# Odd raw weight pieces staged in the turning buffers; the last conversions and the MLP's first half block in one go in slot 21

## The chip, the core and the metric

The kernel runs on one core of a Trainium2 chip. The metric is the device time of one execution in microseconds (us). Runs of one kernel differ by a few us, so results are quoted as medians with their range, and as ratios with a 95% interval.

"Cold" below means that the clock granted to TensorE is half of full, "warm" or "at speed" that it is full. Names: PE is TensorE, PEld its weight loads, DVE VectorE, ACT ScalarE, POOL GpSimd, SP SyncE. L426 is line 426 of the kernel before; in the changed kernel and its variants the numbers can be the same or shifted by one to four.

## The reference

Threshold attention on 8 batches x 8 heads x 576 rows x 64 columns, then a GELU MLP:

```python
scores = scale * (q @ k.T)
thresh = max(scores, axis=-1) - tau
scores = where(scores >= thresh, scores, -1e9)
attn   = softmax(scores)
x      = (attn @ v) as 4608 rows of 512
out    = gelu(x @ w_in) @ w_out           # w_in 512 x 2048, w_out 2048 x 512
```

The weights arrive as 64-bit floats. The kernel turns them into fp32 itself, in 32 pieces of 128 x 512.

## The kernel before

The work is a sequence of 160 *slots*. Slot n = 5p + i handles row tile i of head pair p; four pairs make a batch, so slots 0 to 19 are batch 0, 20 to 39 batch 1. A slot computes scores on PE, reduces, exponentiates and thresholds them (the *softmax*), and turns the result so that it can be multiplied with v. In batch 0 the turning is done on PE; from slot 20 on DVE transposes 32 x 32 blocks into two *turning buffers* `pd`, which are stored to DRAM and fetched back:

```python
pd = [const.tile([P, 4 * KR, P], FP32, name=f"pd{e}") for e in range(2)]
...
def turn_p(p, i):
    ...
    for e in range(n):
        to = pd_tail[p % 2] if i == NC else pd[e][:, :, i * Q:(i + 1) * Q]
        nc.vector.transpose(to[:, 0:NB, :], w[...])
    if i == NC - 1:                      # fourth tile of a pair: store both buffers
        for e in range(2):
            for a in range(4):
                nc.sync.dma_start(s["turned"][e, :, :, a * P:(a + 1) * P], pd[e][a * Q:(a + 1) * Q])
```

The tile of slot n - 1 is turned in slot n, so the buffers are stored in the slots 24, 29, 34 and written again from slots 26, 31, 36 on.

A raw piece is loaded twice by GpSimd, once shifted by three bytes, and converted in steps that alternate between DVE and ACT:

```python
if k % 2 and k < EARLY_PIECES:           # EARLY_PIECES = 24
    room = pd[k // 2 % 2]...             # odd early pieces: staged in a turning buffer
    raw, shifted = room[:, 0:2 * PIECE], room[:, 2 * PIECE:4 * PIECE]
else:                                    # the others: two buffers of the x pool (7 buffers)
    raw, shifted = (xg.tile([P, 2 * PIECE], U32, tag="x", name=s) for s in ("raw", "shifted"))
nc.gpsimd.dma_start(raw, src...)
nc.gpsimd.dma_start(shifted..., src...)
...
vec.tensor_scalar(expo, hi, 0x7FF00000, ...)                 # piece k + 1   0.42 us
nc.scalar.activation(power, expo, AF.Relu, ...)              # piece k + 1   0.72 us
vec.tensor_scalar(mant, top, ...)                            # piece k       0.42 us
vec.scalar_tensor_tensor(power, hi, ..., power, ...)         # piece k       0.69 us
vec.scalar_tensor_tensor(dst, mant, ..., power...)           # piece k       0.69 us
load_piece()                                                 # piece k + 4
```

Steps of the MLP are *filled* in between the slots. A block of 256 rows is 64 `hT` matmuls (two instructions each), a gelu on ACT after every eight of them, and 32 `o_ps` matmuls:

```python
for n in range(len(slots) + WEIGH + 1):
    ...
    scores(p, i); softmax_head(p, i)                 # scores, max, exp
    if 0 < p <= HP and i == 1:
        weigh_v(p - 1, 1); weighed = p               # turned softmax times v, copied to x by ACT
    if 0 < n <= len(slots): turn_p or turn_p_early of slot n - 1
    ...
    if p < NP: softmax_tail(p, i, batch < 2)         # threshold, sum, scaling
    ...
    if batch == 0:
        convert(EARLY_PIECES * 2100 / BATCH)
    elif n < BATCH + 2:
        convert(1e12 if n > BATCH else 9000)         # the last eight pieces, slots 20 and 21
    if batch:
        share = ...
        if batch == 1:
            share = BLK_NS / 8 if n < BATCH + 4 else (share * BATCH - BLK_NS / 2) / (BATCH - 4)
        fill(share, weighed // HP)
    if 0 < p <= HP and i == 0:
        weigh_v(p - 1, 0)
```

## Time and profile before

| | |
|---|---|
| time | 1517.32 us, median of 3 (1515.79 to 1517.84) |
| span of the profiled execution | 1520.2 us |
| PE busy | 1442.4 us (95%) |
| DVE busy | 900.2 us (59%) |
| ACT busy | 640.4 us (42%), with 147 table loads of 1.28 us |

The prediction below shows where PE waits and what ended each wait.

One thing about this trace matters for every later comparison. It has a wait for a load of k at its start that a second trace of the same kernel does not have. PE, in order of time (start, us, instruction, count, idle before and its releaser), first in the profiled execution above:

```profile
30.95 0.36 PE L256 MATMUL tr<-ident,k 64*128 64x64 f32 x1 [3.15 <-DMA k<-in_k_dram]
```

and in the second trace (run `before_2` below):

```profile
28.04 0.27 PE L256 MATMUL tr<-ident,k 64*128 64x64 f32 x1 [0.26 <-DMA k<-in_k_dram]
```

Where two traces are compared below, I therefore count from the start of slot 4's scores, which lies after this wait.

### The profile page before, as it was taken

The page shows a single profiled execution, that of the slowest core. Times are in us where ns is not written, and L with a number is a line of the kernel's source. Part 1 is how long each engine was busy: PE and PEld are TensorE (multiplying, and loading weights), DVE is VectorE, ACT ScalarE, POOL GpSimd, SP SyncE. Part 2 cuts the span into 40 slices and gives each one's busy share as a digit, 9 for nine tenths or more (in the row PEclk, how much of TensorE's full clock was granted, in tenths as well). Part 3 has the DMA queues.
Part 4 walks back from the last instruction along what each step waited for, and adds up shares of the span by engine and source line. Part 5 has one row for each costly group of instructions (what it writes and reads, how often), then busy time and mean ns, then how long its engine had stood idle before and what let it go on. Part 6 is the DMA issues. An engine that isn't in the chain of part 4 may idle for free.

```text
span 1520.2 us, 17439 instructions
## 1 busy us (share of the span) xinstructions
PE 1442.4 (95%) x6092; PEld 899.0 (59%) x6092; DVE 900.2 (59%) x2089; ACT 640.4 (42%) x932; POOL 41.3 (3%) x84
## 2 busy tenths in 40 slices
PE   5877588999999999999999999999999999999998
PEld 3544454656666565656565656575757474765764
DVE  6998566676666676676677766666666676000000
ACT  5766353763445343536252635362626262100110
POOL 3121100000000000000000000000000000000000
PEclk9797798999999999999999999999999999999999
DMA  9875447776666667685777776666666655400000
GB/s 264 249 228 148 160 111 199 192 179 170 170 174 176 183 162 183 165 206 145 193 180 182 186 182 181 175 171 156 165 177 179 173 151 146 134 14 7 7 14 14
DMA packets 398887, 237.61 MB, mean 156 GB/s; under 512 B 230352, under 2 KB 380880, under 8 KB 391632
## 3 DMA queue, kind: packets, MB, share of 16 engines
q1 hardware_dynamic: 391632, 202.96, 51.9%
q0 software_dynamic: 7168, 33.54, 6.5%
q8 instruction: 49, 0.80, 0.2%
q14 instruction: 38, 0.31, 0.1%
HBM read 144.43 MB, written 92.01 MB: 156 GB/s over the span
## 4 chain that ended last, share of the span: by engine, by line
PE 86%; DVE 6%; issue 3%; SPq 2%; ACT 2%; DMA 2%; POOL 0%; POOLq 0%; ACTq 0%; DVEq 0%
PE hT L426 33%; PE o_ps L437 32%; PE sc L320 11%; PE xT L398 9%; DVE p L345 2%; DVE nmx L331 1%; DVE power L174 1%; DMA turned<-pd 1%; DVE w_in L176 1%; DMA k<-in_k_dram 1%; SPq L228 1%; ACT p L332 1%; SPq L224 1%; DVE expo L165 0%; SPq L373 0%
## 5 line engine op out<-in xcount | busy, mean ns | idle before, releaser
L426 PE MATMUL hT<-x,w_in 128*128 128x256 f32 x2304 | 524.0, 385 | 16.4 <-ACT x L407 14.3
L437 PE MATMUL o_ps<-w_out,g 128*128 128x512 f32 x1152 | 515.8, 599 | 0.0
L426 PEld LDWEIGHTS hT<-x,w_in 128*128 128x128 f32 x2304 | 437.3, 192 | 105.2 <-issue 25.9
L331 DVE TENSOR_REDUCE nmx<-sc 128x1 f32<-128x576 f32 x288 | 206.3, 752 | 305.2 <-PE sc L320 304.1
L437 PEld LDWEIGHTS o_ps<-w_out,g 128*128 128x128 f32 x1152 | 215.2, 191 | 259.5 <-issue 255.8
L332 ACT ACTIVATE p<-sc,nmx 128x576 f32<-128x576 f32 x288 | 202.6, 740 | 332.7 <-DVE nmx L331 332.4
L345 DVE SCALAR_TENSOR_TENSOR p<-sc,thr,p 128x576 f32<-128x576 f32 x288 | 220.1, 796 | 11.1 <-ACT p L332 9.9
L320 PE MATMUL sc<-kT,qT 64*128 64x288 f32 x1024 | 186.3, 456 | 30.4 <-DVE p L345 29.9
L320 PEld LDWEIGHTS sc<-kT,qT 64*128 64x128 f32 x1024 | 103.4, 197 | 115.5 <-issue 96.2
L368 DVE STREAM_TRANSPOSE pd<-p 128x576 f32<-128x576 f32 x224 | 162.0, 757 | 13.8 <-DMA turned<-pd 13.5
L398 PE MATMUL xT<-pT,v 128*64 128x288 f32 x1280 | 167.8, 416 | 0.0
L430 ACT ACTIVATE g<-hT 128x512 f32<-128x512 f32 x144 | 84.9, 597 | 126.0 <-PE hT L426 125.1
L398 PEld LDWEIGHTS xT<-pT,v 128*64 128x64 f32 x1280 | 90.5, 140 | 77.8 <-issue 20.5
L356 DVE TENSOR_SCALAR p<-p,rden 128x576 f32<-128x576 f32 x216 | 103.6, 518 | 4.2
L430 ACT ACT_TABLE_LOAD x74 | 94.9, 1283 | 12.7 <-PE hT L426 11.6
L332 ACT ACT_TABLE_LOAD x73 | 93.7, 1283 | 3.1 <-DVE nmx L331 1.7
L407 ACT COPY x<-xT 128x256 f32<-128x256 f32 (+7 forms) x128 | 29.2, 284 | 150.4 <-PE xT L398 150.4
L440 ACT COPY o_sb<-o_ps 128x512 f32<-128x512 f32 x36 | 21.0, 583 | 147.4 <-PE o_ps L437 147.4
L354 ACT ACTIVATE p<-p,rden 128x576 f32<-128x576 f32 x72 | 52.3, 769 | 61.7 <-DVE rden L350 61.5
L320 PE MATMUL sc<-kT,q_tail 128*128 128x288 f32 x128 | 42.0, 454 | 13.0 <-DVE p L345 13.0
L320 PEld LDWEIGHTS sc<-kT,q_tail 128*128 128x128 f32 x128 | 22.9, 198 | 30.3 <-issue 26.4
L335 DVE TENSOR_SCALAR thr<-nmx,tau_eff 128x2 f32<-128x2 f32 (+1 forms) x160 | 36.2, 226 | 5.7
(65 smaller groups left out, 420.9 us busy)
## 6 DMA issues: line engine op xcount, KB each, us to landing
pT<-turned SPq DMA_DIRECT2D x56, 1440.0 KB, 8.0
turned<-pd SPq DMA_DIRECT2D x224, 320.0 KB, 5.2
out_dram<-o_sb SPq DMA_DIRECT2D x36, 256.0 KB, 2.2
turned<-pd_tail SPq DMA_DIRECT2D x112, 80.0 KB, 2.9
q<-in_q_dram SPq DMA_DIRECT2D x112, 72.0 KB, 9.0
k<-in_k_dram SPq DMA_DIRECT2D x112, 72.0 KB, 3.2
v<-in_v_dram SPq DMA_DIRECT2D x168, 40.0 KB, 2.2
raw<-in_moe_w_out_dram POOLq DMA_DIRECT2D x12, 512.0 KB, 3.9
```

What stands on the lines that cost most here:

```text
L320: nc.tensor.matmul(sc[e][:, h, 0:HALF], lhsT=lhsT, rhs=s["kT"][rows, at:at + HALF], start=True, stop=True)
L331: nc.vector.tensor_reduce(nmx[:, e:e + 1], sc, axis=AXIS.XY, op=ALU.max, negate=True)
L332: nc.scalar.activation(w[:, e * S:(e + 1) * S].rearrange("p (h s) -> p h s", h=2), sc, AF.Exp, bias=nmx[:, e:e + 1], scale=1.0)
L335: nc.vector.tensor_scalar(thr[:, 0:n], nmx[:, 0:n], -1.0, tau_eff, op0=ALU.mult, op1=ALU.subtract)
L345: nc.vector.scalar_tensor_tensor(row, sc[e][:, :, 0:HALF], thr[:, e:e + 1], row, op0=ALU.is_ge, op1=ALU.mult, accum_out=den[:, e:e + 1])
L354: nc.scalar.activation(row, row, AF.Copy, bias=0.0, scale=rden[:, e:e + 1])
L356: nc.vector.tensor_scalar(row, row, rden[:, e:e + 1], None, op0=ALU.mult)
L368: nc.vector.transpose(to[:, 0:NB, :], w[:, e * S:(e + 1) * S].rearrange("p (b i) -> p b i", i=Q))
L398: nc.tensor.matmul(xT[f, 0:HALF], lhsT=s["v"][:, e, c, :], rhs=pT[:, c, cols], start=(c == 0), stop=(c == KR - 1))
L426: nc.tensor.matmul(hT[:, j % 2, :], lhsT=w_in_sb[c][:, j * P:(j + 1) * P], rhs=x_blk[n][:, c, :], start=(c == 0), stop=(c == N_DM - 1))
L430: nc.scalar.activation(t, hT, AF.Gelu)
L437: nc.tensor.matmul(o[:, 0:d_model], lhsT=g[j][:, m * P:(m + 1) * P], rhs=w_out_sb[j], start=(j == 0), stop=(j == N_DF - 1))
```

## The change

The intent: keep four pieces in flight to the end by staging all odd pieces in the turning buffers; this is allowed only if every conversion is issued before slot 21 writes a turning buffer. So the last conversions move to the middle of slot 21, ahead of `turn_p`, and half a block of the MLP is put behind them to keep PE busy meanwhile. What is left of the filling of batch 1 is spread over slots 22 to 39.

```diff
-        if k % 2 and k < EARLY_PIECES:
+        if k % 2:
...
             weigh_v(p - 1, 1)
             weighed = p
+            if p == HP:
+                convert(1e12)
+                fill(BLK_NS / 2, 1)
...
-        elif n < BATCH + 2:
-            convert(1e12 if n > BATCH else 9000)
-        if batch:
+        elif n > BATCH + 1:
...
-                share = BLK_NS / 8 if n < BATCH + 4 else (share * BATCH - BLK_NS / 2) / (BATCH - 4)
+                share = (goal[1] - 0.5) * BLK_NS / (BATCH - 2)
```

## The prediction

> **What bounds the kernel now.** I read the page first: TensorE (PE) is busy 1442.4 of 1520.2 us, so 77.8 us of idle time is all that a reordering can win. The slices of 38 us say where it lies, the first line being TensorE, the second the clock granted to it:
>
> ```profile
> PE   5877588999999999999999999999999999999998
> PEclk9797798999999999999999999999999999999999
> ```
>
> The idle time is in the first seven or eight slices; the fifth (152 to 190 us) is half empty. So I took busy times by stretch (columns: stretch; its length; then PE, weight loads, VectorE, ScalarE, GpSimd busy, with instruction counts; clock, DMA share, GB/s):
>
> ```profile
> 0.00:150.00 150.00, 105.29 (x508) 67.13 (x510) 127.56 (x319) 97.54 (x172) 34.63 (x72) 0.84 0.75 222
> 150.00:190.00 40.00, 23.55 (x99) 17.36 (x96) 20.05 (x40) 13.10 (x22) 6.66 (x13) 0.76 0.48 165
> 190.00:330.00 140.00, 127.11 (x517) 78.29 (x517) 90.34 (x209) 84.72 (x116) 0.00 (x0) 0.91 0.65 164
> 330.00:1520.20 1190.20, 1186.42 (x4976) 736.24 (x4974) 662.22 (x1522) 445.00 (x624) 0.00 (x0) 1.00 0.56 147
> ```
>
> PE idles 44.7 us in the first batch (before 150), 16.5 us at the seam between batch 0 and batch 1 (150 to 190), 12.9 us in most of batch 1, and 3.8 us after 330. From 330 on PE is the bound. The seam, on PE, in order of time (start, us, what, idle before and its releaser):
>
> ```profile
> 153.10 1.56 PE L426 MATMUL hT<-x,w_in 128*128 128x256 f32 x6
> 169.01 14.41 PE L426 MATMUL hT<-x,w_in 128*128 128x256 f32 x58 [14.35 <-ACT x L407]
> 185.52 0.81 PE L426 MATMUL hT<-x,w_in 128*128 128x256 f32 x2 [2.10 <-ACT g L430]
> ```
>
> The MLP's first block starts, finds its input x missing and waits 14.35 us for a ScalarE copy of 0.3 us. Why was the copy late? ScalarE shows it:
>
> ```profile
> 153.19 0.72 ACT L166 ACTIVATE power<-expo,rebias 128x512 uint32<-128x512 uint32 x1 [3.09 <-DVE expo L165]
> ...
> 167.97 0.72 ACT L166 ACTIVATE power<-expo,rebias 128x512 uint32<-128x512 uint32 x1 [4.22 <-DVE expo L165]
> 168.60 0.44 ACT L407 COPY x<-xT 128x256 f32<-128x256 f32 x2
> ```
>
> It stands in program order behind conversions of weight pieces, which wait for VectorE, which waits for DMA. GpSimd, which issues the loads, waits in its turn for a staging buffer:
>
> ```profile
> 158.59 0.53 POOL L143 DMA_DIRECT2D raw<-in_moe_w_out_dram  x1 [3.73 <-DVE mant L172]
> 159.19 0.54 POOL L145 DMA_DIRECT2D shifted<-in_moe_w_out_dram  x1
> 163.57 0.53 POOL L143 DMA_DIRECT2D raw<-in_moe_w_out_dram  x1 [3.85 <-DVE mant L172]
> ```
>
> From piece 24 on both buffers of every piece come from the x pool (7 buffers, 3 of them held by x itself), so only two pieces are in flight and one turn of load, convert, load takes 5.0 us (158.59 to 163.57), though a conversion occupies VectorE for only 2.1 us (0.34+0.34+0.7+0.7, start to start).
>
> **What the Trainium skill says.** "DMA: Bandwidth & Descriptors", section "Anatomy of one DMA — SWDGE (gpsimd) path", fits 2.0 us plus bytes/436 GB/s: 3.2 us for 512 KB. The trace has 3.9 us for `raw` and 4.6 for `shifted` from issue to landing, so latency, not bandwidth, paces the turn: the DMA share is 0.48 at the seam. "SBUF — State Buffer", "SBUF: two separate sides", warns that GpSimd can't write descriptors while VectorE runs a two-port instruction; the trace cannot show the lock, but in the busy first batch such loads still land after a median of 3.8 to 6.5 us by group. "TensorE: Matmul & The Clock Gate", Part 1, says an idle window of about 3.4 us halves the clock. The trace agrees: after a 4.18 us wait at 223.48 eight score instructions take 2.99 us instead of 1.24, and the next eight `o_ps` 5.64 instead of 3.70. "ScalarE: Activation LUTs", "What ACT_TABLE_LOAD costs", gives 1283 ns for the load itself; the trace shows 1.28 us, 147 of them.
>
> **The change, part by part.**
> (a) *Odd pieces from 25 on are staged in the turning buffers.* No instruction is added. Pieces 24 to 27 are then all landed before slot 21: 25's load can go when piece 21 leaves its buffer (132.5 us), 27's when piece 23 does (142.7).
> (b) *Slot 20 converts nothing; the rest runs in slot 21, after the copies of x and ahead of the slot's VectorE tail.* On ScalarE the x copies now precede seven `power` steps, so x is there when PE finishes the weighing at 153.1.
> (c) *The first half block, all 64 `hT` matmuls (128 instructions), runs at once there.* Four PSUM buffers take 64 instructions, 64 x 0.24 = 15.4 us, to about 168.5, before the first gelu is needed.
> Conversions: scores of slot 21 end at 149.3, VectorE reduces them by 150.5, then eight pieces x 2.1 us = 16.8, plus about 1 us because `power` of piece 25 waits for the last x copy (153.7): end near 168.5. Loads 28 to 31 are triggered near 151.5, 154.3, 155.9, 158.5 and land some 5 us later, hardly late. The last `power` is done near 165.4; one table load, 1.28: the first gelu ends at 167.3, before PE fills its fourth buffer. So PE runs from 153.1 for 128 x 0.24 = 30.7 us to 183.8 and goes on to slot 22's scores. Before, PE had 66 of the 128 done at 188.47 after those scores. After, scores end at 185.1 with all 128 done: 3.4 + 62 x 0.238 = 18.1 us ahead, of which 1.7 us is warm clock.
>
> What is given back. Slot 21's row scaling on ScalarE now stands behind eight gelus (184.4), so slot 22's softmax is a bare chain: scaling to 185.8, table load 187.1, exp 188.5, threshold 189.4, then the q and k turning 193.1, slot 23's reduce 194.6, threshold 197. PE has only two sets of four `o_ps` matmuls (3.7 us each) there: idle about 3.4 us ahead of slot 24, a cold clock after. The second turning of slot 24 starts near 200.0 instead of 206.71. From there the chain is fixed:
>
> ```profile
> 206.71 1.43 DVE L368 STREAM_TRANSPOSE pd<-p 128x576 f32<-128x576 f32 x2
> ...
> 221.85 0.78 DVE L368 STREAM_TRANSPOSE pd<-p 128x576 f32<-128x576 f32 x1 [3.70 <-DMA turned<-pd]
> ...
> 223.48 2.99 PE L320 MATMUL sc<-kT,qT 64*128 64x288 f32 x8 [4.18 <-DVE p L345]
> ```
>
> Eight stores from the turning buffers, issued 1.4 us apart, must land before slot 26 may write them: 15.1 us, whatever PE does. So slot 26's wait ends near 215.1, 6.7 us earlier, and PE's lead beyond that is idle time. But at that point PE has done more than before: 18 `o_ps` matmuls against 13 besides the 64 `hT`, worth 5 x 0.9 = 4.5 us, so slots 27 to 39 get less filling (3.03 instead of 3.41 us nominal). Where PE sets the pace (two filled slots between each buffer wait and the next turning, and the last three slots before batch 2) that shortens the path: 1 `o_ps` (0.9), 2 `hT` (0.9), 2 `hT` (0.9), then about half of the last slots' saving (0.8): 3.5 us. Elsewhere it becomes idle time. Sum: 6.7 + 3.5 = 10.2 us at the start of batch 2; from there both kernels do the same work with PE full.
>
> **Rivals.**
> 1. *The whole lead survives* (16.5 to 18 us, 1500). For it: PE is the bound later. Against: three waits for the turning buffers (4.18, 5.11, 2.42 us) already stand in batch 1 and cannot be shortened by filling PE earlier.
> 2. *The buffer wait swallows nearly all* (2 to 5 us, 1513): if slots 22 and 23 take longer than I think, slot 24's turning moves little. For it: ScalarE and VectorE are serial there. Against: VectorE's work per slot is about 5 us.
> 3. *The burst of loads starves the conversions*: if they land 7.9 us after issue, the worst of the first batch, the last conversion slips by about 3 us and the first gelu with it; PE waits 2 to 3 us: 1510.
> 4. *Seam idle is hidden anyway*: no; nothing else ran on PE at the seam.
>
> **Range and chances.** 1517.3 - 10.2 = 1507.1, rounded to 1507.5 for cold-clock losses. Rivals 1 and 2 set the edges, not quite at their ends: 1501.5 to 1513. Two per cent is 30.3 us, and the 150 to 330 idle time is 29.4 in all, so faster by 2% is nearly excluded; slower by 2% would need a new stall of 30 us.
>
> **What would show it.** In the changed profile: no wait of `hT` for the x copy; one unbroken run of 128 `hT` instructions from 153 to 184; landed loads for pieces 24 to 27 ahead of slot 21 and an end of the conversions at 168 to 170; a new PE wait of 3 to 4 us ahead of slot 24; buffer waits of 4 to 6 us still in slots 26 and 31, the first ending near 215. PE idle near 1 us in 150 to 190, and some 6 us more than now over batch 1. I am wrong if slot 24's turning comes at 205 or later, or if the buffer waits vanish.

## The result, and the profile after

The changed kernel took 1512.15 us in the median (1508.78 to 1513.79, 4 runs), the kernel before 1516.55 us (1515.51 to 1517.84, 4 runs) beside it. The ratio is 0.9968, interval 0.9947 to 0.9988. A ratio is always the mean time of one kernel's fast runs over that of the other's of the same rounds, so it is not quite the ratio of the medians. The gain is about 5 us; predicted were 10.2.

The slices of the page (PE, and the clock granted to it):

```profile
PE   5877878899999999999999999999999999999998
PEclk9798989899999999999999999999999999999999
```

The fifth slice went from 5 to 8. By stretch (length; PE, PEld, DVE, ACT, POOL busy; clock, DMA share, GB/s):

```profile
150.00:190.00 40.00, 36.14 (x149) 27.58 (x148) 22.75 (x46) 15.44 (x22) 4.57 (x8) 0.96 0.29 109
190.00:330.00 140.00, 120.19 (x467) 69.09 (x465) 91.94 (x212) 75.79 (x105) 0.00 (x0) 0.90 0.69 173
330.00:1511.50 1181.50, 1177.69 (x4949) 732.51 (x4948) 656.83 (x1509) 443.79 (x622) 0.00 (x0) 1.00 0.56 147
```

PE's idle time fell from 16.5 to 3.9 us between 150 and 190 and rose from 12.9 to 19.8 us between 190 and 330. The seam on PE:

```profile
148.11 14.08 PE L426 MATMUL hT<-x,w_in 128*128 128x256 f32 x64
165.75 15.77 PE L426 MATMUL hT<-x,w_in 128*128 128x256 f32 x64 [3.56 <-ACT g L430]
181.45 1.24 PE L320 MATMUL sc<-kT,qT 64*128 64x288 f32 x8
```

The wait for the x copy is gone. In its place stands a wait of 3.56 us for the first gelu, after which 64 instructions take 15.77 us instead of 14.08. ACT shows why the gelu is late: the last `power` starts at 163.07, after 3.58 us of waiting for DVE, which had waited for the last load.

```profile
163.07 0.72 ACT L166 ACTIVATE power<-expo,rebias 128x512 uint32<-128x512 uint32 x1 [3.58 <-DVE expo L165]
163.81 1.28 ACT L430 ACT_TABLE_LOAD   x1
165.10 2.07 ACT L430 ACTIVATE g<-hT 128x512 f32<-128x512 f32 x4
```

The turnings and the wait for the buffer, on DVE, in the slots 24 and 26 (their counterparts of before are at 206.71 and 221.85):

```profile
196.94 1.43 DVE L368 STREAM_TRANSPOSE pd<-p 128x576 f32<-128x576 f32 x2
...
212.14 0.78 DVE L368 STREAM_TRANSPOSE pd<-p 128x576 f32<-128x576 f32 x1 [4.43 <-DMA turned<-pd]
```

They lie 15.2 us apart, as before (15.1). What is left of the gain at the end is decided later. PE in slots 38 and 39 of the changed kernel:

```profile
295.44 2.99 PE L320 MATMUL sc<-kT,qT 64*128 64x288 f32 x8 [2.28 <-DVE p L345]
298.36 5.55 PE L426 MATMUL hT<-x,w_in 128*128 128x256 f32 x14
303.84 5.07 PE L398 MATMUL xT<-pT,v 128*64 128x288 f32 x40
308.84 1.24 PE L320 MATMUL sc<-kT,q_tail 128*128 128x288 f32 x4
```

and in slots 37 to 39 of the kernel before:

```profile
298.38 2.99 PE L320 MATMUL sc<-kT,qT 64*128 64x288 f32 x8 [2.42 <-DVE p L345]
301.30 5.75 PE L426 MATMUL hT<-x,w_in 128*128 128x256 f32 x16
306.98 1.24 PE L320 MATMUL sc<-kT,qT 64*128 64x288 f32 x8
308.15 3.72 PE L426 MATMUL hT<-x,w_in 128*128 128x256 f32 x16
311.80 5.07 PE L398 MATMUL xT<-pT,v 128*64 128x288 f32 x40
316.80 1.24 PE L320 MATMUL sc<-kT,q_tail 128*128 128x288 f32 x4
```

Before, slot 38 takes PE 9.8 us. After, PE first waits 2.28 us for slot 37's thresholds, which free the score buffers, and then runs the scores and the `hT` of slot 38 cold (granted clock 0.59 from 295.44 to 303.84): 13.4 us from start to start, with one `hT` matmul (two instructions) less to do. The kernel before pays the same price one slot earlier: it waits 2.42 us ahead of slot 37 and runs that slot at a clock of 0.60 (298.38 to 306.98).

I read the start of each slot's scores from the traces and worked out the *lead*: the distance from slot 4's scores to those of slot n in `before_2`, minus the same distance in the other run. From slot 45 on the lead stays constant within 1 us, since PE is then full.

| lead in us at slot | 22 | 27 | 38 | 41 |
|---|---|---|---|---|
| predicted | 2.5 | 6.7 | 9.4 | 10.2 |
| changed kernel, the trace above | 1.1 | 5.9 | 8.1 | 4.7 |
| changed kernel, trace of `a_again` | 4.2 | 8.1 | 10.8 | 9.1 |
| changed kernel, trace of `a_3` | 1.7 | 6.5 | 9.5 | 6.1 |

(Predicted at slot 22: 186.25 - 183.8; at 38: 6.7 + 3 x 0.9.) Up to slot 27 the prediction stands within the scatter of three traces. From there to slot 41 it expects 3.5 us more; the traces change by -1.3, +1.0 and -0.5. That the leads at slot 38 agree is luck: at slot 36 they are 6.4, 9.1 and 7.8, and the 1.7 us that follow come mostly from the cold slot 37 of the kernel before. The softmax gains nothing there (the table of threshold steps below).

My theory after this reading: (1) the seam is as predicted, but for a late first gelu; (2) slots 34 to 40 are paced by the softmax chain and not by PE, so PE gets short waits there and a cold clock; (3) the half block in one go is too long: DVE sits idle for 13.22 us waiting for slot 22's scores. The rivals: that the gain comes from the start of the run; that reordering without staging does it; that filling PE early is all that counts.

### The profile page after: what moved, and what is told of

It reads as the page before. It is cut to its first block, busy times and chain, and to the rows that moved or that the text cites. A ratio compares the mean times of both kernels' runs of the same rounds, so it can differ in the third digit from the quotient of the medians.

```text
span 1511.5 us, 17425 instructions
## 1 busy us (share of the span) xinstructions
PE 1440.8 (95%) x6092; PEld 897.7 (59%) x6092; DVE 901.7 (60%) x2089; ACT 635.4 (42%) x928; POOL 41.6 (3%) x84
## 4 chain that ended last, share of the span: by engine, by line
PE 83%; DVE 9%; ACT 3%; DMA 2%; SPq 2%; issue 1%; ACTq 0%; DVEq 0%
PE o_ps L437 32%; PE hT L426 31%; PE sc L320 11%; PE xT L398 9%; DVE p L345 3%; DVE nmx L331 2%; DVE power L174 1%; DMA turned<-pd 1%; ACT p L332 1%; DVE expo L165 1%; DVE w_in L176 1%; SPq L228 1%; DVE mant L172 1%; DMA pd<-in_moe_w_out_dram 1%; SPq L224 1%
## 5 line engine op out<-in xcount | busy, mean ns | idle before, releaser
L437 PEld LDWEIGHTS o_ps<-w_out,g 128*128 128x128 f32 x1152 | 215.1, 190 | 260.1 <-issue 257.1
```

What stands on the lines that cost most here:

```text
L437: nc.tensor.matmul(o[:, 0:d_model], lhsT=g[j][:, m * P:(m + 1) * P], rhs=w_out_sb[j], start=(j == 0), stop=(j == N_DF - 1))
```

## The experiments

Twelve runs followed. All gave correct results.

### a_again: the changed kernel once more

No edit.

> The changed kernel itself, unaltered, for a tighter interval. If the gain is real: ratio near 0.997 to before (about 1512 us). If the measured 4 us came from the start of the run (in the profiled run of before, TensorE waited 3.15 us for a load of k at 28 us, in that of after it did not): ratio near 1.000.

Measured: 1513.89 us (1508.82 to 1518.12, 6 runs), before 1517.65 (1516.01 to 1523.06, 11 runs); ratio 0.9965, interval 0.9943 to 0.9987. The gain of about 5 us is real and not the start of the run. In its trace PE waits 2.17 us for the first gelu and stays at speed:

```profile
164.39 14.08 PE L426 MATMUL hT<-x,w_in 128*128 128x256 f32 x64 [2.17 <-ACT g L430]
```

Its lead at slot 41 is 9.1 us, twice that of the first trace of the same program. A single trace is a sample.

### before_2 and a_3: one look each

No edits.

> The kernel before, unaltered, once more, for a second trace. If the wait of 3.15 us for k at 28 us was chance: here slot 3's scores start near 27.8 us instead of 30.96, the later slots keep the same distances (slot 22 some 148.3 us after slot 4), and the span is about 1516.5. Rival (the wait belongs to the kernel before): it is there again.

Measured: slot 3's scores at 28.05 us, slot 22 147.9 us after slot 4, span 1516.3 us. The wait for k was chance; the traces of two variants, `b_order_only` and `e_five_sixteenths`, have it too (2.61 and 2.30 us). It made the profiled span of before 3 us longer than usual; a reader who subtracts the two profiled spans (1520.2 and 1511.5) gets 8.7 us where the timed runs have 5.

> The changed kernel, unaltered, for a third trace. Two traces of it differ by 4.5 us after slot 4: one waited 3.56 us for the first gelu and ran the next 64 hT instructions in 15.77 us, the other waited 2.17 us and took 14.08 us; slot 38 took 13.4 and 11.7 us. Theory (the length of the wait[...] decides): in this trace a wait under about 3 us goes with 14.1 us, a longer one with 15 to 16. Rival: no such link.

Measured: the wait for the first gelu was 3.05 us and the next 64 instructions took 15.64 us. With the other traces of kernels that have the half block in one go: waits of 2.14, 2.17, 2.21 and 2.68 us were followed by 14.08 us, those of 3.05 and 3.56 by 15.64 and 15.77. That agrees with the theory, but see `e_five_sixteenths` for an exception, and the end of the account of the prediction for what decides it. 1512.74 us in its single run.

### b_order_only: the order without the staging

```diff
-        if k % 2:
+        if k % 2 and k < EARLY_PIECES:
```

> The changed order alone: pieces 25, 27, 29 and 31 go back to the x pool, so only two pieces are in flight. Theory (the staging is what makes the conversions short): the turn of load and conversion is 5 us again, the first gelu comes near 182 us instead of 165, TensorE waits some 14 us after 64 hT instructions, and the time is 1520 to 1526. Rival (moving the x copies ahead of the conversions is what counts): as the changed kernel, 1512.

Measured: 1527.9 us (1525.79 to 1530.56, 6 runs), ratio 1.0057 (1.0039 to 1.0074): slower than before. PE:

```profile
183.10 16.98 PE L426 MATMUL hT<-x,w_in 128*128 128x256 f32 x64 [17.16 <-ACT g L430]
```

The first gelu comes at 183 us and PE waits 17.16 us. The rival falls: without the staging the new order loses about 9 us. The time is just above the expected range (1520 to 1526), as the wait was 3 us longer than estimated.

### c_stage_old_fill: staging and early conversion, the filling as before

```diff
-                fill(BLK_NS / 2, 1)
...
-        elif n > BATCH + 1:
+        if batch:
...
-                share = (goal[1] - 0.5) * BLK_NS / (BATCH - 2)
+                share = BLK_NS / 8 if n < BATCH + 4 else (share * BATCH - BLK_NS / 2) / (BATCH - 4)
```

> Staging and the eight pieces ahead of slot 21's tail as changed, but the MLP filled as before (a quarter block at the end of slot 21, an eighth each in 22 and 23, the rest over 24 to 39). Theory (the half block in one go delays the softmax of slots 22 to 26: VectorE sat idle 13.22 us for slot 22's scores): TensorE waits about 10 us for the first gelu, but slot 22's scores start some 10 us earlier than in before, with 66 hT done as in before, and this lead lasts to the end: 1507 to 1509, faster than the changed kernel. Rival (the one go is what won the 4 us): 1513 to 1517.

Measured: 1510.87 us (1508.38 to 1513.64, 6 runs), ratio 0.9948 (0.993 to 0.9965). PE waits 9.67 us for the first gelu, as expected, and has a lead of 7.9 us at slot 22 and 9.1 at 41. The time is about 2 us above the expected range. It is not slower than the changed kernel, so the one go is not what won the gain; that it is faster is not clear, as the intervals of the ratios overlap (0.9943 to 0.9987 there).

### d_late_spread: no filling in slots 22 and 23

```diff
-        elif n > BATCH + 1:
+        elif n > BATCH + 3:
...
-                share = (goal[1] - 0.5) * BLK_NS / (BATCH - 2)
+                share = (goal[1] - 0.5) * BLK_NS / (BATCH - 4)
```

> The changed kernel, but nothing filled in slots 22 and 23 and the remaining block spread over slots 24 to 39 as in before. Theory (slots 22 and 23 are bound by the softmax chain, so their filling is free, but with it one gelu falls into each of slots 34 to 39, where TensorE waits 2.28 us ahead of slot 38 and then runs cold): slot 24 starts when it does in the changed kernel or up to 2 us later for cold clocks, the wait ahead of slot 38 goes, time 1509 to 1511. Rival (the spread is harmless and the loss lies elsewhere): 1512 to 1514.

Measured: 1511.91 us (1508.21 to 1513.83, 6 runs), ratio 0.9953 (0.9936 to 0.997). Inconclusive: it lies between the two ranges. In its trace slot 24 starts at the same lead (9.3 us) as in `a_again`, which shows the filling of slots 22 and 23 to be free there. But the wait ahead of slot 38 did not go; it is 1.84 us. My reason for it (one gelu in each slot because of seven `hT` instead of eight) was wrong: before also has a gelu in each of these slots. What the spread does move is a gelu in slot 31: all traces of the changed kernel have one there, before and this run have none. From the first threshold step of slot 31 to that of slot 32 it is 7.40 us with the gelu and 6.25 us without.

### e_five_sixteenths: a shorter first go

```diff
-                fill(BLK_NS / 2, 1)
+                fill(BLK_NS * 5 / 16 - 100, 1)
...
-                share = (goal[1] - 0.5) * BLK_NS / (BATCH - 2)
+                share = (goal[1] - 5 / 16) * BLK_NS / (BATCH - 2)
```

> The changed kernel, but only five sixteenths of a block (40 hT) run in slot 21 instead of a half (64); the rest is spread over slots 22 to 39. Theory (the one go holds up the softmax: VectorE waits 13.2 us for slot 22's scores): scores of slot 22 start some 8 us earlier than in the changed kernel (near 170 us), those of slot 27 some 4 to 9 us earlier, and part of that is given back by more filling later: 1506 to 1510. Rival (TensorE's work done is all that counts, so the place of filling is neutral): 1512 to 1514.

Measured: 1501.29 us (1499.21 to 1503.72, 5 runs) against 1516.64 (1515.25 to 1520.52, 9 runs); ratio 0.9893 (0.9875 to 0.9912), 16 us faster than before. It is well below the expected range, and its interval lies apart from those of the changed kernel. PE at the seam:

```profile
167.14 5.41 PE L426 MATMUL hT<-x,w_in 128*128 128x256 f32 x16 [2.07 <-ACT g L430]
172.48 1.24 PE L320 MATMUL sc<-kT,qT 64*128 64x288 f32 x8
```

The lead is 13.0 us at slot 22, 17.8 at 27 and 19.8 at 41. So the one go had held up the softmax of slots 22 to 26, and the work that PE puts off costs nothing later: the lead even grows. The turning of slot 24 comes at 188.3 us (on the time scale of before, 206.7 there and 200.2 in the changed kernel) and slot 26's wait for the buffers ends at 203.5 instead of 215.4: the stores take 15.2 us here too, but start 12 us earlier. The rival (the place of filling is neutral) falls. The first line is also the exception announced above: after a wait of only 2.07 us, 16 instructions took 5.41 us, where they take 3.72 at speed.

### f_wait_slots: more filling where PE waits for the turning buffers

```diff
 (on top of e_five_sixteenths)
+        early_fill = batch == 1 and i == 1 and p > HP
+        if early_fill:
+            fill(2.36 * (goal[1] - 5 / 16) * BLK_NS / (BATCH - 2), 1)
...
-        elif n > BATCH + 1:
+        elif n > BATCH + 1 and not early_fill:
...
+                share = 0.728 * (goal[1] - 5 / 16) * BLK_NS / (BATCH - 2)
```

> As e_five_sixteenths, but the filling of slots 22 to 39 is uneven: slots 26, 31 and 36, in which TensorE waits 4 to 6 us for the turning buffers, get 2.36 shares, ahead of VectorE's part of the slot, and the others 0.73. Theory (those waits are fixed in length, so only work put inside them is free[...]): the waits ahead of slots 27, 32 and 37 fall below 2 us, slots after them run warm, and the time is 1497 to 1503. Rival (the longer slots 26 and 31 delay the next turning and all is even): 1506 to 1510, as e_five_sixteenths.

Measured: 1502.54 us (1501.63 to 1503.48, 4 runs), ratio 0.99 (0.9883 to 0.9916): within the expected range at its upper edge, but no faster than `e_five_sixteenths`. The wait ahead of slot 32 fell to 0.51 us and those ahead of 27 and 37 went. In exchange slots 26 and 36 became longer: the 40 `hT` instructions in slot 36 took 10.59 us, and the lead ends at 15.1 us from slot 41 on, against 19.8 in `e_five_sixteenths` (17.3 at slot 36, 12.9 at 37, 16.3 at 38). The rival's mechanism (the longer slots take back what the waits gave) was right here; its number was not, as it stood for `e_five_sixteenths` before that was measured.

### h_memset_early: the memsets out of the conversions

```diff
-        if p < HP + 4:
+        if p < HP + 2:
             nc.gpsimd.memset(t, 0.0)
+        elif p == HP + 3:
+            nc.vector.memset(t, 0.0)
...
+        if n == BATCH - 2:
+            nc.gpsimd.memset(v_sb[2], 0.0)
```

> The changed kernel with the two GpSimd memsets of v that run in the midst of slot 21's conversions moved away (one to slot 18, one to VectorE in slot 26). In all traces the mant step of piece 28 takes 1.87 us instead of 0.42 while they run. Theory ([...]hidden, since the loads of pieces 28 to 31 move 4.2 MB in some 13 us and the last one decides): that step takes 0.42 us, the wait for the last load grows by as much, TensorE still waits 2 to 3.5 us for the first gelu, time unchanged, 1511 to 1514. Rival (the memsets cause that wait): TensorE's wait falls to 1 us or less and the time to 1508 to 1510.

Measured: 1510.49 us (1507.51 to 1517.26, 4 runs), before 1519.95 (1517.57 to 1521.53, 9 runs), ratio 0.9948 (0.9925 to 0.997). The `mant` step of piece 28 on DVE, in the changed kernel and then in this run:

```profile
155.14 1.87 DVE L172 TENSOR_SCALAR mant<-shifted 128x512 uint32<-128x512 uint32 x1
```

```profile
155.96 0.42 DVE L172 TENSOR_SCALAR mant<-shifted 128x512 uint32<-128x512 uint32 x1
```

The step is as short as its siblings when the memsets are elsewhere, so they did stretch it. But DVE now waits for the loads instead, 1.38 us ahead of piece 30 and 1.30 ahead of 31 (lines `expo`), and PE still waits 2.68 us for the first gelu. The loads decide when the first gelu comes. Why the memsets stretch the step no run shows. Whether the time fell is open: its ratio overlaps those of the changed kernel.

### j_slot37: filling moved from slot 39 to slot 37

```diff
-            fill(share, weighed // HP)
+            fill(share * {37: 1.6, 39: 0.4}.get(n, 1.0), weighed // HP)
```

> The changed kernel with slot 37's share of filling raised by 0.6 and slot 39's lowered by 0.6 (12 and 2 hT matmuls instead of 7 and 7). Theory (half of what was predicted is lost in slot 38, where TensorE waits 2.28 us for the softmax chain and then runs cold): the wait ahead of slot 38 falls below 1 us, slots 38 and 39 start warm, and the lead over before at slot 40, counted from slot 4, rises from 4.9 to 9.3 us in the three traces to 9 to 11: 1507 to 1510. Rival (what is lost there comes back somewhere else, or the two table loads and a second gelu lengthen the chain): 1511 to 1514.

Measured: 1510.67 us (1509.99 to 1512.69, 5 runs), ratio 0.9944 (0.9932 to 0.9957). The wait ahead of slot 38 is gone, slots 38 and 39 run at speed, and the lead rises to 14.7 us at slot 40. That figure flatters: the first two of the slot's eight score instructions start early, and the other six wait. By the first threshold step the lead at slot 40 is 11.2 us. Then part of it is lost again in slot 40, on PE:

```profile
307.88 2.25 PE L320 MATMUL sc<-kT,qT 64*128 64x288 f32 x6 [3.46 <-DVE p L345]
310.06 8.17 PE L437 MATMUL o_ps<-w_out,g 128*128 128x512 f32 x14
```

PE waits 3.46 us for a threshold and then runs slowly (14 `o_ps` instructions take 6.28 us at speed). The lead at slot 41 is 8.3 us, no more than in the best trace of the changed kernel. So the mechanism is right (a wait, then a cold clock), but the wait belongs to the chain of the softmax and only changed its place when PE's work was moved: the rival was right about that, though the time lies between the two ranges.

### i_three_eighths: a first go between the two

As `e_five_sixteenths`, with 3/8 in place of 5/16.

> The changed kernel with three eighths of a block (48 hT) in slot 21, between e_five_sixteenths (40) and the changed kernel (64). Theory (each hT matmul of the one go beyond the time at which slot 22's scores may start delays the softmax by 0.22 to 0.24 us an instruction, and only part comes back): 1503 to 1508. Rival (40 was a lucky alignment): 1510 to 1514.

Measured: 1502.68 us (1501.5 to 1504.89, 4 runs) against 1519.95 of before, ratio 0.9892 (0.9878 to 0.9905): as good as 40 matmuls, so no lucky alignment; below the expected range by 0.3 us. Slot 22's scores start at 171.82, against 178.40 in `a_again`; 16 matmuls of two instructions at 0.22 us are 7.0 us. The last sixteen `hT` matmuls of the half block cost about 11 us in time (0.9965 against 0.9892 of some 1517 us; 1512.74 for the single run `a_3` against 1501.29 for `e_five_sixteenths`).

### k_two_queues: half of the stores issued by GpSimd

```diff
 (on top of e_five_sixteenths)
+                q_store = nc.gpsimd if e and p < 2 * HP else nc.sync
-                    nc.sync.dma_start(s["turned"]...)
+                    q_store.dma_start(s["turned"]...)
```

> e_five_sixteenths with the four stores of the second turning buffer issued by GpSimd instead of SyncE in batch 1. Theory (the 14.5 us from a pair's last turning to the release of the second buffer is mostly eight issues of 1.4 us in a row on one queue): the release comes some 4 to 6 us earlier, the waits ahead of slots 32 and 37 go, and the time is 1495 to 1500. Rival (the transfers themselves are the limit, or the descriptors on GpSimd are as slow): 1500 to 1503.

Measured: 1505.42 us (1504.82 to 1508.8, 5 runs), ratio 0.9913 (0.9899 to 0.9927). A miss: not faster, and above both expected ranges. The issues did get quicker, 2.70 us for the four of GpSimd. But the transfers took longer. From issue to landing (KB each, median us), between 185 and 225 us:

```profile
turned<-pd SPq DMA_DIRECT2D x5, 320.0 KB, 4.6
turned<-pd POOLq DMA_DIRECT2D x4, 320.0 KB, 7.9
turned<-pd_tail SPq DMA_DIRECT2D x4, 80.0 KB, 7.3
```

Over all 16 stores of GpSimd and 16 of SP, landing took up to 12.9 us. From the pair's last turning to the release it is 16.2 us (185.40 to 201.55), where `e_five_sixteenths` has 14.5 (187.97 to 202.46). Whether the transfers or the descriptors are slow was not separated.

## Why the prediction was right or wrong

The range (1501.5 to 1513) held. The gain was predicted twice too large. Point by point, with 3.3 us added to the times of the first changed trace, for its earlier start (34.66 against 37.93 at slot 4):

**Right: what bounds the seam.** The x copy behind the conversions was the cause; the wait is gone in all traces of the changed order. `b_order_only` shows that the staging is needed for it.

**Right: the conversions.** Predicted end 168.5; measured 169.5 (166.22 + 3.3), and 168.0 in `a_again`.

**Wrong in part: "the first gelu ends at 167.3, before PE fills its fourth buffer".** It ends at 169.0, and PE fills its four buffers in 14.08 us rather than 15.4. So the unbroken run of 128 instructions did not come about: PE waited 2.2 to 3.6 us. The mis-sized term was "land some 5 us later, hardly late". Eight transfers were triggered within 7.7 us, 4.2 MB in all, and by group they landed after medians of 5.0 to 7.2 us. The prediction had read "latency, not bandwidth" from a DMA share of 0.48 at the seam. That does not carry over to the burst: between 150 and 160 us of the changed trace the DMA engines are busy for 0.99 of the time and move 374 GB/s. Its figures for "the busy first batch" (3.8 to 6.5 us by group, 7.9 at worst) are those of 60 to 150 us; over all of 0 to 150 us the groups have medians of 3.8 to 8.7 us and single loads up to 13.9. `h_memset_early` shows that the other suspect, the memsets, does not decide it. Rival 3 of the prediction named this, with about the right size.

**Right: what is given back in slots 22 to 26.** The turning of slot 24 was predicted for 200.0 and came at 200.2; the buffer wait of slot 26 for 215.1 and ended at 215.4 (198.1 and 213.2 in `a_again`, 199.6 and 214.8 in `a_3`). That it fits so closely is in part luck: 128 instructions at 0.24 us were counted where 0.22 was measured (2.6 us too many), and the wait for the first gelu was left out (2.2 to 3.6 us too few). The wait ahead of slot 24 was 2.59 us (predicted 3.4). Idle time of 150 to 190 was 3.9 us (predicted near 1), that of 190 to 330 rose by 6.9 (predicted 6).

**Wrong: the 3.5 us that less filling was to save "where PE sets the pace".** The sum was 6.7 + 3.5. The 6.7 came true: the leads at slot 27 are 5.9, 8.1 and 6.5 us. Of the 3.5 nothing is left on average: from slot 27 to 41 the leads change by -1.3, +1.0 and -0.5 us. From slot 27 to 40 the first threshold step of a slot on DVE follows that of the slot before after the same time, within 0.05 us, in seven of thirteen cases, although PE has less to do in the changed kernel. PE does not set the pace there; the softmax does. The last of these threshold steps start at these times:

| slot | 36 | 37 | 38 | 39 | 40 |
|---|---|---|---|---|---|
| before | 297.44 | 304.84 | 313.05 | 321.17 | 327.18 |
| after | 287.02 | 294.46 | 302.67 | 313.02 | 319.04 |

The distances are 7.4, 8.2, then 8.1 against 10.4, then 6.0 in both. The 7.4 us is a ring through two engines: two thresholds (1.6), sum and reciprocal (0.4), scaling (1.4), a table load (1.3), one gelu (0.6), a table load (1.3), the first exp (0.7), which are 7.3 with the steps rounded. ACT loads a table whenever it changes between exp and gelu. The 8.2 us have the scaling of the next q (0.8) in the ring besides. Filling less work into such a slot saves nothing; it only lets PE wait.

Part by part: the 0.9 us of slots 27 and 28 came true (8.5 us from slot 28 to 29 in `before_2`, 7.7, 7.5 and 7.3 in the changed kernel). Those of slots 32 and 33 did too (9.1 us from slot 33 to 34, then 8.1), but the gelu that now falls into slot 31 took back 1.15. The rest, 0.9 + 0.8 for the last slots, became a loss. Of the distances in the table, only from slot 38 to 39 does DVE wait long for PE (3.10 us before, 5.52 after), and just there PE is cold after its wait of 2.28 us: this distance grows by 2.2, 0.6 and 2.2 us in the three traces. Slot 38 took PE 13.4, 11.7 and 13.4 us, and that is part of the scatter of the changed kernel's times. Another part is the late gelu with its cold clock (3.1 us at slot 22 between the first two traces). These parts are read from traces, and no run changed one of them alone, but for the last: `j_slot37` takes the wait out of slot 38, the distance from slot 38 to 39 is 8.1 us again, and the wait turns up in slot 40. The trace of the kernel before held a warning: its third wait, 2.42 us ahead of slot 37, was followed by a cold clock, while the prediction looked at the one of 4.18 us alone.

**Not asked: whether a half block was the right amount.** I counted the 18 us of work that PE gets ahead as a gain, and what the softmax loses meanwhile as a price that I took for unavoidable. `e_five_sixteenths` and `i_three_eighths` show that it is avoidable: with 40 or 48 matmuls in place of 64 the kernel gains 16 us, three times as much. Slot 22's scores could start at about 169 (its buffers are free when the thresholds of slot 21 end, 169.0 in the changed trace); every `hT` after that delays the softmax of slots 22 to 26, for idle time of PE that comes back later anyway.

Two questions can be settled from the traces. Why does PE run cold after a wait of 2.1 us and not after one of 2.7? In all 14 traces the granted clock keeps one value for whole multiples of 3.41 us, so the trace falls into stretches of that length. In `e_five_sixteenths` the wait of 2.07 us lies in a single stretch (columns as above, lengths in us):

```profile
164.70:168.11 3.41, 1.34 (x6) 0.87 (x5) 3.34 (x7) 3.38 (x6) 0.00 (x0) 1.00 0.10 25
168.11:171.53 3.42, 3.42 (x10) 2.66 (x9) 2.71 (x8) 0.45 (x1) 0.00 (x0) 0.50 0.00 0
```

In `f_wait_slots` the longer wait, 2.70 us, is split between two:

```profile
162.85:166.26 3.41, 1.62 (x8) 1.09 (x6) 2.26 (x5) 1.75 (x2) 0.00 (x0) 1.00 0.35 109
166.26:169.68 3.42, 2.50 (x12) 2.22 (x13) 3.38 (x6) 2.32 (x5) 0.00 (x0) 1.00 0.00 0
```

PE is busy for 0.39 of the first stretch of `e_five_sixteenths`, and the next one is cold; it is busy for 0.48 and 0.73 in `f_wait_slots`, and the clock stays. Ten traces have a wait of 2.0 to 3.6 us for the first gelu. In the three that went cold after it the least busy stretch had 0.17, 0.20 and 0.39; in the seven others 0.44 to 0.66. So the place of a wait counts as much as its length, and it differs from trace to trace. As a general border this is not sharp: over all stretches up to 330 us, those with a busy share between 0.41 and 0.65 were followed by either clock.

Why is the timed gain of `e_five_sixteenths` (15.4 us between the medians) below its lead of 19.8? Its trace has the wait for k at the start, which the lead leaves out: slot 4 starts at 37.57 us against 34.93 in `before_2`, so 17.2 us remain. And `before_2`, with 1518.09 us, was 1.5 us above the median of its call.

In `e_five_sixteenths` the spread of the later filling changes along with the first go. Where the spread alone was changed, the median moved by 2 us (`d_late_spread` against `a_again`) and by 1 us (`f_wait_slots` against `e_five_sixteenths`), so most of the 11 us is due to the first go. What stays open: what made the stores of `k_two_queues` land later, and what stretches the `mant` step while the memsets run.

## What to carry to other kernels

When work is moved into a gap, fill only until the next link of the longest chain can start: here 40 to 48 matmuls gained 16 us and 64 gained 5, although PE was the engine at 95%. A slot with a ring of waits between two engines has its own pace, and taking work from a third engine there wins nothing; look for that pace as equal distances between the same instructions in both traces. Compare traces from a common event after the start, and take a second trace before explaining a difference of 3 us. When a lead is read from one engine, check it on the engine that sets the pace: PE's lead at slot 38 looked right by chance.

## What the Trainium skill lacked or had wrong

- "TensorE: Matmul & The Clock Gate", Part 1, ties the halved clock to an idle window of about 3.4 us. The traces agree with the length (the clock changes in steps of 3.41 us), but a window need not be wholly idle: in `e_five_sixteenths` the clock halved after a window in which PE was idle for 2.07 us (0.61 of it), while a wait of 2.70 us in `f_wait_slots`, split over two windows, left the clock up. In the changed kernel even a wait of 1.60 us ahead of slot 36 was followed by a cold stretch (14 `hT` in 4.97 us in place of 3.29).
- "DMA: Bandwidth & Descriptors", "Anatomy of one DMA — SWDGE (gpsimd) path", gives a time for one DMA; the estimate from it for 512 KB is 3.2 us. With eight in flight the medians were 5.0 to 7.2 us, at a DMA share of 0.99; the section has no figure for that.
- I found no page with a price for issuing stores of many small rows. Eight stores of 320 KB took SyncE 1.4 us each to issue, 10.3 us in a row; half of them issued by GpSimd took 0.7 us each, but landed after 7.9 us instead of 5.1.
